# Attention, Fourier mixing and two channel mixers on one core: the softmax reciprocals go to the feature layout through TensorE, not through DRAM

## The chip, the cores and the metric

One core of a Trainium2 chip runs the whole kernel in one launch. The metric is device time in microseconds, median of three runs; less is better.

## What is computed

Three layers follow each other over 4 batches of 576 positions with 8 heads of 64 features (512 features in all). The change touches the end of the first one.

```python
scores = scale * np.matmul(q, k.transpose(0, 1, 3, 2)) + decay   # decay from the running sum of log f, causal
attn = np.exp(scores - np.max(scores, axis=-1, keepdims=True))
attn = attn / (np.sum(attn, axis=-1, keepdims=True) + 1e-09)
x = np.matmul(attn, v)                       # [B, H, S, D], then to [B, S, 512]
u = x + np.real(fft(fft(x, axis=1), axis=2))
x = u + np.maximum(layernorm(u) @ w_ch1, 0.0) @ w_ch2
theta = x @ w_theta                          # then the second mixer, cos, sin, token and channel weights
```

## The kernel before, in words

The kernel has three phases. Phase 1 is attention over 32 heads, in 16 pairs, with the Fourier layer of a batch woven in after its four pairs; phase 2 is the first channel mixer; phase 3 the second mixer. Only phase 1 is touched, and the profile shows attention from about 10 to 366 us.

For each head `score_units` works through five blocks of 128 queries (the last block is queries 448 to 575, of which the last 64 are new). TensorE makes scores in PSUM (L232, L233), VectorE masks them and takes the row minimum (L240), ScalarE exponentiates them into the tile `P` with the row sums as a by-product in `zs` (L245). After the second head of a pair VectorE adds the pieces of the sums and takes the reciprocals (L250 to L254), giving `rz`, with queries on partitions: `[128, 2 heads, 5 blocks]`. `turn_units` transposes the exponentials on TensorE (L275) and copies them out of PSUM with ScalarE (L279) or, for the first of four banks, VectorE (L281). `av_units` multiplies them with `v` in the PSUM tile `T` (L297), in which features of both heads lie on partitions and queries run along the row. So the scaling needs the reciprocals along the row, the same for 64 partitions at a time: the tile `R`, `[128, 576]`.

In the kernel before, `rz` gets there through DRAM. Four stores on SP's DMA queue (L257, L258) write one element at a time into `row`, two lines of 576 numbers; two loads (L485) read each line back with a broadcast to 64 partitions. They are issued at the start of the step that begins the product with `v`, two heads after the sums. `evac_pair` then multiplies `T` by `R` on VectorE into `X` (even pair, L313) or `Y` (odd pair, L319). For an odd pair three small copies on SP's queue move single rows of `Y` about (L322 to L329), GpSimd clears one row (L324), and GpSimd makes `E = X + Y` and `O = X - Y` (L332, L334), from which `fft_units` makes the Fourier layer.

SP's queue also carries, in the order of the program, the loads of heads (`raw`, L191, two buffers, 576 KB) and of `v` (L186). An instruction on that queue that waits holds those behind it. `prep_units` starts each head: ScalarE rounds `raw` to `hi` (L200), GpSimd takes the remainder (L201), and so on to L211, on VectorE.

A scheduler in the language orders the instructions of each engine, by emission and a priority: scores have 20 and the product with `v` 40 instructions of advance. The buffers that matter are `T` (one, of two PSUM banks), `R` (one), `X` (one), the slot `ol` (one, shared by `Y` and a tile of `fft_units`), and three PSUM banks of `bank_b`, which the transposes, the Fourier layer and the layer norm share. `phase1` advances the generators of transposes, product with `v` and scores in turn, about six rounds a head.

Of the kernel before, what the change touches and what calls it, by code (L numbers as in the profile page):

```python
# [8 lines left out]
F32 = mybir.dt.float32  # L9
# [4 lines left out]
ALU = mybir.AluOpType  # L14
# [3 lines left out]
B, H, S, D = 4, 8, 576, 64  # L18
NP = 4
# [36 lines left out]
class Net:  # L56
# [159 lines left out]
    def score_units(self, hd, g):  # L216
        nc = self.nc
        hi, kl, q2 = hd["hi"], hd["pair"]["kl"], self.q2[g]
        P = self.w3.tile([128, 1856], F32, tag="P", name="P", bufs=2)
        mn = self.w3.tile([128, 8], F32, tag="mn", name="mn", bufs=2)  # L220
        pr = hd["g"] // 2
        zs, rz = self.zs[pr % 2], self.rz[pr % 2]
        hd["P"] = P
        for i in (4, 3, 2, 1, 0):
            n0 = TOP[i]
            q = slice(n0, n0 + 128)
            ps = self.bank_a()
            pd = self.bank_a() if i == 4 else None
            parts = [(ps, 0, n0), (pd, n0, n0 + 128)] if i == 4 else [(ps, 0, n0 + 128)]
            with self.tc.high_priority(20):  # L230
                for t, a, b in parts:
                    nc.tensor.matmul(t[:, 0 : b - a], hi[:, 1, q], hi[:, 0, a:b], start=True, stop=False)  # L232
                    nc.tensor.matmul(t[:, 0 : b - a], q2[:, q], kl[:, g, a:b], start=False, stop=True)  # L233
                if i < 4:
                    dg, w, init = ps[:, 0 : n0 + 128], n0 + 128, 3.0e38
                else:
                    dg, w, init = pd[:, 0:128], 128, mn[:, 5:6]
                    nc.vector.tensor_reduce(init, ps[:, 0:n0], mybir.AxisListType.X, ALU.min)
                lowest = mn[:, i : i + 1]
                nc.vector.tensor_tensor_reduce(  # L240
                    out=dg, in0=dg, in1=self.mask[:, S - w : S], scale=1.0, scalar=init,
                    op0=ALU.add, op1=ALU.min, accum_out=lowest,
                )
                for k, (t, a, b) in enumerate(parts):
                    nc.scalar.activation(  # L245
                        P[:, POFF[i] + a : POFF[i] + b], t[:, 0 : b - a], AF.Exp, bias=lowest,
                        scale=-1.0, accum_out=zs[:, g, i + k : i + k + 1],
                    )
            if i == 0 and g:
                nc.vector.tensor_scalar(rz[:, :, 0:4], zs[:, :, 0:4], 1e-9, None, ALU.add)  # L250
                nc.vector.scalar_tensor_tensor(
                    rz[:, :, 4:5], zs[:, :, 4:5], 1e-9, zs[:, :, 5:6], ALU.add, ALU.add
                )
                nc.vector.reciprocal(rz[:, :, 0:5], rz[:, :, 0:5])  # L254
                row = self.fdram.tile([2, S], F32, tag="row", name="row", bufs=2)
                for k in range(2):
                    nc.sync.dma_start(row[k : k + 1, 0:512].rearrange("o (i p) -> p (o i)", p=128), rz[:, k, 0:4])  # L257
                    nc.sync.dma_start(row[k : k + 1, 512:S].rearrange("o p -> p o"), rz[64:128, k, 4:5])  # L258
                hd["pair"]["row"] = row
            yield  # L260

    def turn_units(self, hd):
# [18 lines left out]
                nc.vector.tensor_copy(dst, ps[:, 0:w])  # L281
            yield

    def av_units(self, hds, T, done):
        nc = self.nc
        v = hds[0]["pair"]["v"]
        place = {(j, a): PTOFF[bank] + off for bank, pieces in enumerate(TURNED) for j, a, b, off in pieces}
        yield
        for js in ((0, 1), (2, 3, 4)):
            with self.tc.high_priority(40):  # L290
                for j in js:
                    for lo_q, hi_q in ((0, 256), (256, 576)):
                        a = max(lo_q, 128 * j)
                        if a >= hi_q:
                            continue
                        for g, hd in enumerate(hds):
                            nc.tensor.matmul(  # L297
                                T[64 * g : 64 * g + 64, 256 + a : 256 + hi_q],
                                v[:, j, g, :],
                                hd["PT"][:, place[j, a] : place[j, a] + hi_q - a],  # L300
                                start=j == 0,
                                stop=j == 4 or (j == 1 and hi_q == 256),
                            )
            for _ in range(5 if js[0] == 0 else 1):
                yield
        done()

    def evac_pair(self, p, R, T):
        nc = self.nc
        k = p // 2  # L310
        if p % 2 == 0:
            self.X = self.c1.tile([128, S], F32, tag="X", name="X", bufs=1)
            nc.vector.tensor_tensor(self.X, T[:, 256:832], R, ALU.mult)  # L313
            if k == 0:
                self.EO = [self.c1.tile([128, 2, S], F32, tag=x, name=x, bufs=2) for x in ("E", "O")]
            return
        X, (E, O) = self.X, self.EO
        Y = self.c1.tile([128, S], F32, tag="ol", name="Y", bufs=1)
        nc.vector.tensor_tensor(Y, T[:, 256:832], R, ALU.mult)  # L319
        if k == 0:  # L320
            self.x384 = self.fdram.tile([1, S], F32, tag="x384", name="x384", bufs=2)
            nc.sync.dma_start(self.x384, Y[64:65])  # L322
            nc.sync.dma_start(Y[64:65], Y[0:1])
            nc.gpsimd.memset(Y[0:1], 0.0)  # L324
        else:
            self.x256 = self.c1.tile([1, S], F32, tag="x256", name="x256", bufs=1)
            nc.sync.dma_start(self.x256, Y[64:65])
            nc.sync.dma_start(Y[64:65], Y[0:1])
            nc.sync.dma_start(Y[0:1], self.x384)  # L329
        for _ in range(4):  # L330
            yield
        nc.gpsimd.tensor_tensor(E[:, k], X, Y, ALU.add)  # L332
        yield
        nc.gpsimd.tensor_tensor(O[:, k], X, Y, ALU.subtract)  # L334
        yield
# [104 lines left out]
    def phase1(self):  # L440
        pair, heads = self.p1_open()
        NH = B * H
        pairs, heads, raws = {0: pair}, dict(enumerate(heads)), {}
        fft = None
        self.tick = 0
        rows, norm, av = iter(()), iter(()), iter(())
# [19 lines left out]
        for n in range(-1, NH + 1):  # L466
# [13 lines left out]
            m, odd = divmod(n - 2, 2)  # L480
            if m >= 0 and not odd:
                T = self.bank_t()
                R = self.w3.tile([128, S], F32, tag="R", name="R", bufs=1)
                for k in range(2):
                    self.nc.sync.dma_start(R[64 * k : 64 * k + 64], pairs[m]["row"][k : k + 1].to_broadcast([64, S]))  # L485
                av = self.av_units([heads[2 * m], heads[2 * m + 1]], T, lambda m=m, T=T, R=R: done(m, T, R))
            t = self.turn_units(heads[n]) if 0 <= n < NH else iter(())
            if n == NH - 1:
                self.p1a.close()
# [692 lines left out]
```

## Time and profile before

| What | Value |
|---|---|
| Median of 3 runs | 1097.87 us (1094.99 to 1103.09) |
| Profiled execution, its time | 1099.61 us |
| Its span, first to last instruction | 1097.8 us |
| Mean granted TensorE clock | 0.937 |
| TensorE matmuls busy | 970.4 us (88%) |
| VectorE, ScalarE, GpSimd busy | 649.4, 450.8, 500.1 us |

The profile is one execution, taken apart by instruction. Times of rows are microseconds from the first instruction. A busy TensorE need not run at its full rate: the granted clock says how much of it the chip allowed, 1.00 or half of that at a time, and a mean between them says how the stretch was divided. Idle time of an engine is put down to what released it last. L numbers are lines of the kernel before.

### The profile page before, as it was taken

To read this page: it belongs to the slowest core of one execution; us is meant where nothing else is said; L and a number is where in the kernel's file an instruction comes from. 1 tells how busy PE (TensorE), PEld (TensorE's weight loads), DVE (VectorE), ACT (ScalarE), POOL (GpSimd) and SP (SyncE) were. 2 spreads that over 40 slices of the span, in tenths; PEclk is the share of its full clock that TensorE was granted. 3 is DMA by queue.
4 is the path that set the end of the run, shared out by engine and by line. 5 is a ranking of instruction groups with operands and counts; after the bars stand their busy time and mean duration, and the time that the engine had idled before them with its cause. 6 is when DMAs were issued, how large, how long until landed. Compare 5 with 4: busy or idle time off the path is not lost. (4 is left out here: it accounts for less than half of the span.)

```text
span 1097.8 us, 16258 instructions
## 1 busy us (share of the span) xinstructions
PE 970.4 (88%) x5880; PEld 874.3 (80%) x5880; DVE 649.4 (59%) x1429; ACT 450.8 (41%) x1128; POOL 500.1 (46%) x534
## 2 busy tenths in 40 slices
PE   4578898869879558999989999999999999999998
PEld 3355566546656347999989999999999999999998
DVE  7454765666756497875345533653467675665654
ACT  5355654554644443433123322422244453434431
POOL 5334523433535476664226541653266663635421
PEclk9878988979989777899999999999999999999999
DMA  4765444526343422100012123213342000000001
GB/s 148 121 119 89 112 63 93 98 69 79 71 74 46 88 77 69 48 1 5 35 40 100 53 86 108 77 54 126 116 143 66 1 1 23 22 23 23 12 33 44
DMA packets 46355, 72.85 MB, mean 66 GB/s; under 512 B 23502, under 2 KB 26958, under 8 KB 46276
## 3 DMA queue, kind: packets, MB, share of 16 engines
q1 hardware_dynamic: 42436, 67.32, 24.1%
q0 software_dynamic: 3120, 3.33, 2.3%
q10 hardware_dynamic: 720, 1.18, 0.3%
q8 instruction: 46, 0.75, 0.3%
q14 instruction: 33, 0.27, 0.1%
HBM read 62.64 MB, written 9.14 MB: 65 GB/s over the span
## 5 line engine op out<-in xcount | busy, mean ns | idle before, releaser
L740 PE MATMUL pa<-un,wf 128*128 128x384 f32 x1152 | 225.1, 343 | 24.2 <-POOL wf L568 12.5
L740 PEld LDWEIGHTS pa<-un,wf 128*128 128x128 f32 x1152 | 205.7, 192 | 27.6 <-POOL wf L568 13.6
L746 DVE SCALAR_TENSOR_TENSOR h<-pa,h 128x384 fp32r<-128x384 f32 x96 | 53.0, 555 | 166.7 <-ACT h L745 166.7
L754 PE MATMUL pb<-h,wf 128*128 128x384 f32 x660 | 138.2, 342 | 3.5 <-ACT h L745 3.1
L232 PE MATMUL pa<-hi 128*128 128x448 f32 (+2 forms) x192 | 77.6, 411 | 71.4 <-ACT P L245 58.0
L245 ACT ACTIVATE P<-pa,mn 128x512 f32<-128x512 f32 (+2 forms) x192 | 97.8, 517 | 89.4 <-DVE mn L240 65.8
L754 PEld LDWEIGHTS pb<-h,wf 128*128 128x128 f32 x660 | 118.7, 192 | 5.6 <-ACT h L745 3.8
L232 PEld LDWEIGHTS pa<-hi 128*128 128x128 f32 x192 | 41.8, 218 | 90.3 <-ACT P L245 56.1
L745 ACT ACTIVATE h<-pa 128x384 fp32r<-128x384 f32 x96 | 46.8, 489 | 154.6 <-PE pa L740 154.4
L754 PE MATMUL po<-h,wf 128*128 128x384 f32 x492 | 105.3, 343 | 2.5 <-DVE u L762 1.7
L961 PE MATMUL pb<-wtk,z 128*128 128x288 f32 x513 | 97.0, 294 | 0.0
L275 PE MATMUL pb<-ident,P 128*128 128x128 f32 x480 | 90.4, 307 | 6.4 <-DVE yl L392 6.0
L297 PE MATMUL pt<-PT,v 128*64 128x320 f32 (+4 forms) x448 | 94.5, 406 | 1.5 <-ACT PT L279 1.5
L951 POOL TENSOR_TENSOR z<-kra,z 128x256 fp32r<-128x256 f32 x72 | 53.9, 768 | 88.1 <-ACT z L950 88.1
L754 PEld LDWEIGHTS po<-h,wf 128*128 128x128 f32 x492 | 89.3, 193 | 4.0 <-ACT h L745 2.1
L565 POOL TENSOR_TENSOR a<-a,wf 128x512 f32<-128x512 f32 x32 | 42.2, 1321 | 106.7 <-DVE t L564 102.9
L275 PEld LDWEIGHTS pb<-ident,P 128*128 128x128 f32 x480 | 64.5, 156 | 28.8 <-issue 17.4
L240 DVE CUSTOM_DVE_ANT_0 pa<-pa,mask 128x512 f32<-128x512 f32 (+3 forms) x128 | 62.6, 504 | 36.6 <-PE pa L233 33.3
L961 PEld LDWEIGHTS pb<-wtk,z 128*128 128x128 f32 x513 | 79.2, 188 | 0.0
L961 PE MATMUL po<-wtk,z 128*128 128x288 f32 x351 | 75.1, 295 | 2.2 <-ACT z L950 1.6
L233 PE MATMUL pa<-kl,q 66*128 66x448 f32 (+2 forms) x192 | 68.8, 371 | 1.2 <-DVE kl L211 1.2
L201 POOL TENSOR_TENSOR hi<-raw,hi 64x576 fp32r<-64x576 f32 x31 | 45.4, 1466 | 45.1 <-ACT hi L200 40.5
(206 smaller groups left out, 1932.9 us busy)
## 6 DMA issues: line engine op xcount, KB each, us to landing
raw<-in_qk SPq DMA_DIRECT2D x31, 576.0 KB
raw<-in_wf SPq DMA_DIRECT2D x32, 512.0 KB
raw<-in_wtk SPq DMA_DIRECT2D x18, 288.0 KB
v<-in_vp SPq DMA_DIRECT2D x16, 320.0 KB
R<-row SPq DMA_DIRECT2D x32, 144.0 KB
out<-ob SPq DMA_DIRECT2D x12, 288.0 KB
dft<-in_dft POOLq DMA_DIRECT2D x8, 346.0 KB, 11.8
raw<-in_wth SPq DMA_DIRECT2D x4, 512.0 KB
```

What stands on the lines that cost most here:

```text
L232: nc.tensor.matmul(t[:, 0 : b - a], hi[:, 1, q], hi[:, 0, a:b], start=True, stop=False)
L233: nc.tensor.matmul(t[:, 0 : b - a], q2[:, q], kl[:, g, a:b], start=False, stop=True)
L240: nc.vector.tensor_tensor_reduce(out=dg, in0=dg, in1=self.mask[:, S - w : S], scale=1.0, scalar=init, op0=ALU.add, op1=ALU.min, accum_out= ...
L245: nc.scalar.activation(P[:, POFF[i] + a : POFF[i] + b], t[:, 0 : b - a], AF.Exp, bias=lowest, scale=-1.0, accum_out=zs[:, g, i + k : i + k ...
L275: nc.tensor.transpose(ps[:, o : o + 128], src, self.ident)
L297: nc.tensor.matmul(T[64 * g : 64 * g + 64, 256 + a : 256 + hi_q], v[:, j, g, :], hd["PT"][:, place[j, a] : place[j, a] + hi_q - a], start= ...
L740: nc.tensor.matmul(ps[:, 0:CH], t[:, l, 128 * d : 128 * d + 128], un[r][:, d], start=n == 0, stop=n == 11)
L745: nc.scalar.activation(h[:, 0], ps[:, 0:CH], AF.Relu)
L746: nc.vector.scalar_tensor_tensor(h[:, 1], ps[:, 0:CH], 0.0, f(h[:, 0]), ALU.max, ALU.subtract)
L754: nc.tensor.matmul(outs[d], t[:, l, 128 * d : 128 * d + 128], h[:, r], start=k % G == 0 and n == 0, stop=k % G == G - 1 and n == 2,)
L951: nc.gpsimd.tensor_tensor(z[:, 1], t, f(z[:, 0]), ALU.subtract)
L961: nc.tensor.matmul(acc[k][th], z[:, l, 128 * k : 128 * k + 128], self.wtk[kt][:, r, 288 * th : 288 * th + 288], start=first and i == 0 and ...
```

## The change

The stores, the tile `row` and the loads of `R` go. In `score_units`, after the reciprocals, GpSimd spreads `rz` into a new tile `wide`, `[128, 5 blocks, 128]`, in which each reciprocal of head 0 stands 64 times and each of head 1 64 times (one instruction, one buffer). In `av_units`, ahead of the second group of products with `v` of the pair, the new `spread` transposes the five blocks on TensorE, four of them into a bank of `bank_b` and the fifth into unused columns of `T`, and ScalarE copies them (512 columns and 64 columns) into `R`. `R` now stands in the slot of `X` or of `Y`, and the multiply of `evac_pair` writes over it.

```diff
--- before.py
+++ after.py
@@ -252,11 +252,12 @@
                     rz[:, :, 4:5], zs[:, :, 4:5], 1e-9, zs[:, :, 5:6], ALU.add, ALU.add
                 )
                 nc.vector.reciprocal(rz[:, :, 0:5], rz[:, :, 0:5])
-                row = self.fdram.tile([2, S], F32, tag="row", name="row", bufs=2)
-                for k in range(2):
-                    nc.sync.dma_start(row[k : k + 1, 0:512].rearrange("o (i p) -> p (o i)", p=128), rz[:, k, 0:4])
-                    nc.sync.dma_start(row[k : k + 1, 512:S].rearrange("o p -> p o"), rz[64:128, k, 4:5])
-                hd["pair"]["row"] = row
+                wide = self.w3.tile([128, 5, 128], F32, tag="wide", name="wide", bufs=1)
+                each = rz[:, :, 0:5].rearrange("p g i -> p i g").unsqueeze(3).to_broadcast([128, 5, 2, 64])
+                nc.gpsimd.tensor_scalar(
+                    wide.rearrange("p i (g c) -> p i g c", g=2), each, 1.0, 1.0, ALU.mult, ALU.mult
+                )
+                hd["pair"]["rz"] = wide
             yield
 
     def turn_units(self, hd):
@@ -281,12 +282,25 @@
                 nc.vector.tensor_copy(dst, ps[:, 0:w])
             yield
 
-    def av_units(self, hds, T, done):
+    def spread(self, p, T, wide):
+        nc = self.nc
+        R = self.c1.tile([128, S], F32, tag="ol" if p % 2 else "X", name="Y" if p % 2 else "X", bufs=1)
+        ps = self.bank_b()
+        for i in range(5):
+            to = T[:, 0:128] if i == 4 else ps[:, 128 * i : 128 * i + 128]
+            nc.tensor.transpose(to, wide[:, i], self.ident)
+        nc.scalar.copy(R[:, 0:512], ps)
+        nc.scalar.copy(R[:, 512:S], T[:, 64:128])
+        return R
+
+    def av_units(self, m, hds, T, wide, done):
         nc = self.nc
         v = hds[0]["pair"]["v"]
         place = {(j, a): PTOFF[bank] + off for bank, pieces in enumerate(TURNED) for j, a, b, off in pieces}
         yield
         for js in ((0, 1), (2, 3, 4)):
+            if js[0]:
+                R = self.spread(m % NP, T, wide)
             with self.tc.high_priority(40):
                 for j in js:
                     for lo_q, hi_q in ((0, 256), (256, 576)):
@@ -303,19 +317,19 @@
                             )
             for _ in range(5 if js[0] == 0 else 1):
                 yield
-        done()
+        done(m, T, R)
 
     def evac_pair(self, p, R, T):
         nc = self.nc
         k = p // 2
         if p % 2 == 0:
-            self.X = self.c1.tile([128, S], F32, tag="X", name="X", bufs=1)
-            nc.vector.tensor_tensor(self.X, T[:, 256:832], R, ALU.mult)
+            self.X = R
+            nc.vector.tensor_tensor(R, T[:, 256:832], R, ALU.mult)
             if k == 0:
                 self.EO = [self.c1.tile([128, 2, S], F32, tag=x, name=x, bufs=2) for x in ("E", "O")]
             return
         X, (E, O) = self.X, self.EO
-        Y = self.c1.tile([128, S], F32, tag="ol", name="Y", bufs=1)
+        Y = R
         nc.vector.tensor_tensor(Y, T[:, 256:832], R, ALU.mult)
         if k == 0:
             self.x384 = self.fdram.tile([1, S], F32, tag="x384", name="x384", bufs=2)
@@ -480,10 +494,7 @@
             m, odd = divmod(n - 2, 2)
             if m >= 0 and not odd:
                 T = self.bank_t()
-                R = self.w3.tile([128, S], F32, tag="R", name="R", bufs=1)
-                for k in range(2):
-                    self.nc.sync.dma_start(R[64 * k : 64 * k + 64], pairs[m]["row"][k : k + 1].to_broadcast([64, S]))
-                av = self.av_units([heads[2 * m], heads[2 * m + 1]], T, lambda m=m, T=T, R=R: done(m, T, R))
+                av = self.av_units(m, [heads[2 * m], heads[2 * m + 1]], T, pairs[m]["rz"], done)
             t = self.turn_units(heads[n]) if 0 <= n < NH else iter(())
             if n == NH - 1:
                 self.p1a.close()
```

## Rows read from the trace of the kernel before

**Rows 1.** the page: busy us (share of span) xinstructions by engine

```profile
PE 970.4 (88%) x5880; PEld 874.3 (80%) x5880; DVE 649.4 (59%) x1429; ACT 450.8 (41%) x1128; POOL 500.1 (46%) x534
```

**Rows 2.** windows: length, busy us of PE, PEld, DVE, ACT, POOL, granted clock

```profile
28.00:116.00 88.00, 63.10 (x334) 42.93 (x333) 43.10 (x127) 44.06 (x136) 33.48 (x35) 0.83 0.66 115
116.00:202.00 86.00, 75.14 (x415) 54.37 (x415) 52.87 (x143) 46.76 (x143) 34.75 (x39) 0.86 0.43 87
202.00:293.00 91.00, 72.48 (x417) 52.20 (x417) 56.08 (x145) 46.31 (x143) 33.40 (x37) 0.89 0.47 81
293.00:360.00 67.00, 56.95 (x321) 39.48 (x320) 42.34 (x115) 34.08 (x105) 29.99 (x34) 0.95 0.34 51
```

**Rows 3.** timeline of TensorE: start, us, instruction [idle before it <-releaser]

```profile
54.89 0.80 PE L232 MATMUL pa<-hi 128*128 128x512 f32 x1 [12.05 <-ACT P L245]
...
76.58 0.47 PE L232 MATMUL pa<-hi 128*128 128x128 f32 x1 [6.44 <-ACT P L245]
...
97.17 0.47 PE L232 MATMUL pa<-hi 128*128 128x128 f32 x1 [3.81 <-ACT P L245]
...
138.51 0.71 PE L232 MATMUL pa<-hi 128*128 128x448 f32 x1 [4.12 <-ACT P L245]
...
222.64 0.80 PE L232 MATMUL pa<-hi 128*128 128x512 f32 x1 [6.71 <-ACT P L245]
...
243.94 0.47 PE L275 MATMUL pb<-ident,P 128*128 128x128 f32 x1 [6.04 <-DVE yl L392]
...
276.51 0.44 PE L232 MATMUL pa<-hi 128*128 128x384 f32 x1 [3.21 <-ACT P L245]
...
312.90 0.47 PE L232 MATMUL pa<-hi 128*128 128x128 f32 x1 [6.18 <-ACT P L245]
```

**Rows 4.** timeline of VectorE, the multiply by R, same columns

```profile
53.32 0.76 DVE L313 TENSOR_TENSOR X<-pt,R 128x576 f32<-128x576 f32 x1 [12.18 <-DMA R<-row]
...
75.61 0.76 DVE L319 TENSOR_TENSOR Y<-pt,R 128x576 f32<-128x576 f32 x1 [8.02 <-DMA R<-row]
...
96.60 0.76 DVE L313 TENSOR_TENSOR X<-pt,R 128x576 f32<-128x576 f32 x1 [4.26 <-DMA R<-row]
```

**Rows 5.** timeline of ScalarE, the first rounding of a head

```profile
242.48 0.67 ACT L200 CAST hi<-raw 128x576 fp32r<-128x576 f32 x1 [6.70 <-DMA raw<-in_qk]
...
308.94 0.67 ACT L200 CAST hi<-raw 128x576 fp32r<-128x576 f32 x1 [5.62 <-DMA raw<-in_qk]
```

**Rows 6.** waits, 0 to 500 us: us in total, times, longest us

```profile
ACT hi L200 <- DMA raw<-in_qk: 35.0, 6, 8.4
...
POOL Y L324 <- DMA Y<-Y: 24.6, 3, 11.7
...
DVE X L313 <- POOL O L334: 8.0, 2, 6.6
```

**Rows 7.** waits of the SP queue, 0 to 500 us

```profile
SPq L485 <- DMA row<-rz: 98.3, 21, 9.2
```

**Rows 8.** timeline of the SP queue: last row store, next R loads

```profile
157.08 0.51 SPq L258 DMA_DIRECT2D row<-rz  x1
...
171.10 2.48 SPq L485 DMA_DIRECT2D R<-row  x2
```

**Rows 9.** the page: DMA packets by size

```profile
DMA packets 46355, 72.85 MB, mean 66 GB/s; under 512 B 23502, under 2 KB 26958, under 8 KB 46276
```

**Rows 10.** timeline of TensorE: runs of transposes, x is their number

```profile
68.63 1.09 PE L275 MATMUL pb<-ident,P 128*128 128x128 f32 x8
...
98.62 1.27 PE L275 MATMUL pb<-ident,P 128*128 128x128 f32 x5
```

**Rows 11.** window of the transposes alone: length, PE, PEld, clock, DMA

```profile
150.00:175.00 25.00, 5.13 (x32) 3.81 (x32) 1.00 0.52 48
```

**Rows 12.** lines by form, ScalarE, 28 to 375 us: count, busy, mean ns, idle

```profile
L279 ACT COPY PT<-pb 128x512 f32<-128x512 f32 x31 | 18.1, 584 | 10.9 <-PE pb L275 9.2 <-PE pa L233 1.5
```

**Rows 13.** lines by form, GpSimd, 28 to 375 us

```profile
L204 POOL TENSOR_SCALAR hi<-raw 128x576 fp32r<-128x576 f32 x7 | 4.7, 669 | 23.4 <-issue 14.6 <-PE pa L233 6.6 <-PE pa L232 2.2
```

## What was predicted

> **What bounds the kernel now.** I read the page first: TensorE is busy for 88% of the span and no other engine for more than 59% [rows 1]. That share is a mean over stages, so the next view is the windows over attention, the only stage that the change touches. From 28 to 360 us TensorE is busy for 63.10, 75.14, 72.48 and 56.95 us in windows of 88, 86, 91 and 67 us [rows 2], 267.7 of 332, so 64.3 us idle; its mean granted clock is 0.83 to 0.95, while no other engine reaches 64%. Attention is bound by TensorE with holes in it, and the question is who makes the holes.
>
> The timeline of TensorE has eight idle times of more than 3 us there [rows 3]. They sum to 12.05 + 6.44 + 3.81 + 4.12 + 6.71 + 6.04 + 3.21 + 6.18 = 48.6 us, three quarters of the 64.3. All are put down to ScalarE or VectorE, so the third step is to ask what those stood behind. Just before the first three VectorE stood for 12.18, 8.02 and 4.26 us in the multiply by R, until R had landed [rows 4]; masks and minima queue behind that multiply, the exponentials wait for the minima, and the scores for the PSUM banks. At the sixth and eighth hole ScalarE stood 6.70 and 5.62 us for the data of a head [rows 5]; six such waits sum to 35.0 us [rows 6]. The rest go back to E and O on GpSimd, which stood 24.6 us for the small copies of Y, and for which the X multiply stood 8.0 [rows 6].
>
> Heads and copies of Y share SP's queue with the stores and loads of the reciprocals. That queue stood 98.3 us in front of the R loads because the row stores had not landed, 9.2 us at the longest [rows 7]. One case: the last store is issued at 157.08 and the R loads only from 171.10 on [rows 8]. Head loads and copies behind them on the queue are issued later by as much. The row stores are also many: each pair writes 2 × (512 + 64) = 1152 single numbers, 16 pairs 18,432, which is most of the 23,502 packets under 512 B [rows 9].
>
> **What goes.** Six DMAs a pair, 96 in all, and the stand on SP's queue. I take the holes one kind at a time.
> - The first three, 22.3 us, end with R landing [rows 3, 4]. No DMA makes R afterwards: all of it goes.
> - The other five, 26.3 us, come from heads and copies of Y that are late [rows 3, 5, 6]. These DMAs remain, but no store of single numbers is in front of them. A head still waits for its buffer, and three copies of Y still follow one another, so not all goes. Bounds 0 and 26.3; I take 70%, 18 us.
> - The clock. Full and half speed are the two levels (2.4 and 1.2 GHz), so a mean c means a share 2(1 − c) at half: 29.9 + 24.1 + 20.0 + 6.7 = 80.7 us at half clock [rows 2]. If all 64.3 us of idle time lie in it, 16.4 us of work ran at half clock; if none, 80.7. Work at half clock costs half of its time, so 8 to 40 us are lost. Right after the third hole a run of transposes takes 0.25 us each, another run 0.14 [rows 10], so work behind a hole does run slowly. I put the loss near 18 us and give back two thirds with the holes: 12 us.
>
> Together −52 us.
>
> **What comes.**
> - TensorE: five transposes of 128x128 a pair, 80 in all. Eight in a run took 1.09 us, five took 1.27 us at the lower clock [rows 10]: 0.14 to 0.25 us each, 11 to 20 us. Between the holes TensorE is the bound, so it is paid in full; I take 14.
> - A rule speaks against this term. The Trainium skill (TensorE: Matmul & The Clock Gate, Part 4, PE-mode transpose) says that the full clock does not engage for transposes, which do not count as activity in the same way. The trace only half agrees: a window of 25 us with 32 transposes in it ran at a granted clock of 1.00 throughout [rows 11], with other matmuls between them. By the rule this term would be 20 us instead of 14.
> - ScalarE: copies of 512 and 64 columns from PSUM. The first takes 0.58 us [rows 12], the second between nothing and that: 0.58 to 1.17 us a pair, 9 to 19 in all, on an engine busy 44.06 of 88 us [rows 2]. If TensorE's remaining work covers it, it costs nothing; without cover all 19. Behind these copies stand exponentials, for which scores wait; I take 4.
> - GpSimd: one pass over 640 elements on 128 partitions. 576 elements took 0.67 us [rows 13], so 0.74 us, 12 in all; if the broadcast costs double, 24. GpSimd is busy 33.48 of 88 us [rows 2], so its idle time covers it: 0. Without that cover up to 24, since the remainder of the next head (L201) stands behind it. It also takes up a new wait, for the reciprocals and, with one buffer of wide, for the transposes of the pair before; the pair has two heads of time for it, so 0 again, within the same 24.
> - VectorE: the multiply now waits for two copies on ScalarE. They are emitted ahead of the last products with v, whose run covers them: 0. If the priority of the products puts the transposes behind them, that cover is gone and one copy chain a pair stays, 1.2 us × 16 = 19.
> - SP's queue is only relieved. It keeps heads, v and the copies of Y.
>
> Together +18 us. The sum is 1099.6 − 52 + 18 = 1065.6 us on the profiled execution, whose own time (1099.61) lies 1.7 us above the median of the runs (1097.87): 1064 us.
>
> **Rivals.**
> 1. *The holes go whole.* All eight holes and 30 us of the clock are won, the transposes run at the full clock and the copies are covered: −48.6 − 30 + 11 = −68, 1030 us. For it: SP's stand is 98.3 us, twice the holes [rows 7]. Against it: the buffers of raw and the chain of Y copies stay.
> 2. *Other waits fill the holes.* Only the three R holes go, with the price of their clock unrecovered because the chain scores, minimum, exponential refills the time: −22 + 18 = −4, 1094 us. For it: every hole is released by ScalarE or VectorE [rows 3], which the change does not speed up. Against it: those engines are busy for half to two thirds of the windows [rows 2] and were held by DMAs at the holes.
> 3. *Slower: the slot of R.* R now takes the slot of X or ol when the copy on ScalarE is written, not at the multiply. O of the pair before reads X and Y, so the copy can stand for it, on the engine of the exponentials. Before, VectorE stood at this place 8.0 us in two cases, 6.6 at the longest [rows 6]. If the 16 pairs stand 4.4 us each, that is 70 us: −52 + 18 + 70 = +36, 1134 us. It decides from 34 / 16 = 2.1 us a pair. Against it: O is late mostly through the copies of Y, 24.6 us of them [rows 6], and these come sooner.
> 4. *The clock does not come back.* The time won is filled with transposes and TensorE stays as long at the lower level: the transposes cost 20 us and the 12 us of clock are not won, −40 + 24 = −16, 1082 us. The window at 1.00 with 32 transposes in it speaks against it [rows 11]. The Trainium skill's rule on transposes (above) would give this case.
>
> **How the numbers follow.** Chances: forecast 0.52 (1045 to 1080), holes whole 0.15, other waits 0.13, no clock 0.10, slower 0.10. About 1% is what a measurement of this kernel can tell from no change. Faster by more, below 1086.9, are the forecast, the whole holes and the case without the clock: 0.77, and I leave 0.02 of that to the middle. Within 1%: other waits and that rest, 0.15. Slower: 0.10. The range leaves out the slow case and the upper part of the first rival: 1030 to 1096. It takes in the full 19 us of the copies or the 24 us of GpSimd on top of the sum (1083 or 1088). The likeliest case's own range is 1045 to 1080.
>
> **What would show it.** Right: no R loads in the waits, packets under 512 B near 23,502 − 18,432 = 5070, the wait of ScalarE for heads well under 35.0 us, GpSimd's wait for copies of Y under 10, the granted clock of the attention windows above 0.9, and the end of attention some 30 us earlier with the phases behind it unchanged in length. Wrong: new idle time on ScalarE before the copies into R released by O, or on GpSimd before wide released by the transposes; holes of TensorE of the old size with other releasers; a granted clock no higher although the holes are fewer.

## The result and the profile after

| | before | changed |
|---|---|---|
| median, same chip | 1100.11 us | 1014.61 us (1011.74 to 1016.53, 4 runs) |
| changed to before | | 0.9225, 95% interval 0.9180 to 0.9271 |
| the profiled execution, its span | 1099.61, 1097.8 us | 1011.74, 1010.0 us |

The kernel became 85.5 us faster; 34 were forecast (1064 against 1097.87), and 1014.61 lies below the range of 1030 to 1096. The direction is as predicted, and most of the gain lies in attention as predicted; the size is not.

The page of the changed kernel, engines and packets, beside [rows 1, 9] (PE is TensorE, PEld its loading of weights, DVE VectorE, ACT ScalarE, POOL GpSimd, SPq SP's queue):

```profile
PE 927.5 (92%) x5960; PEld 855.4 (85%) x5960; DVE 649.8 (64%) x1429; ACT 460.2 (46%) x1160; POOL 511.0 (51%) x550
...
DMA packets 24339, 68.06 MB, mean 67 GB/s; under 512 B 3534, under 2 KB 6990, under 8 KB 24260
```

TensorE's busy time fell by 42.9 us although it has 80 instructions more. Nothing that it did before was taken away, so its instructions became shorter or overlap more. The packets under 512 B fell by 19,968, more than the 18,432 numbers of the row stores; the other 1,536 are exactly 16 for each of the 96 DMAs that went. (Part 4 puts 64 of these DMAs back, and 19,456 packets under 512 B with them: the 18,432 numbers and again 16 for each DMA.)

Two windows of the changed kernel, from 28 us to the last product with v and from there to the end (columns: length; busy us of PE, PEld, DVE, ACT, POOL, each with its count; granted clock, DMA share, GB/s):

```profile
28.00:294.50 266.50, 238.83 (x1621) 180.18 (x1620) 199.68 (x540) 189.03 (x575) 146.41 (x164) 0.99 0.32 97
294.50:1010.00 715.50, 676.47 (x4295) 664.91 (x4294) 429.64 (x846) 254.57 (x545) 350.61 (x354) 0.97 0.16 53
```

The same two of the kernel before, whose last product with v ends at 370.8 us, somewhat later than the end of attention named ahead of the prediction:

```profile
28.00:370.80 342.80, 277.28 (x1536) 196.30 (x1535) 197.91 (x534) 176.84 (x538) 135.64 (x148) 0.87 0.48 85
370.80:1097.80 727.00, 681.36 (x4299) 668.28 (x4299) 431.40 (x850) 257.15 (x550) 350.41 (x354) 0.97 0.17 55
```

Attention went from 342.8 to 266.5 us, 76.3 of the 87.8 us by which the span is shorter. There TensorE's idle time went from 65.5 to 27.7 us, its busy time from 277.28 to 238.83 us with 85 instructions more (the 80 transposes; a few records are missing from a trace), and its granted clock from 0.87 to 0.99. The stages behind are 11.5 us shorter. (The changed kernel was profiled a second time, with every engine's instructions in the same order: attention was 267.0 us and the stages behind 718.5, so a difference of 3 us between two profiles means nothing.)

The waits of the changed kernel, 0 to 420 us (us in total, times, longest us):

```profile
ACT P L245 <- DVE mn L240: 59.5, 43, 7.6
...
POOL Y L338 <- DMA Y<-Y: 3.5, 2, 2.4
...
ACT X L292 <- POOL O L348: 3.5, 3, 1.8
POOL wide L257 <- PE pb L291: 3.4, 3, 2.6
```

ScalarE's wait for a head's data, 35.0 us before [rows 6], is no longer among them: what ScalarE waits for most is the minima of VectorE, 59.5 us, that is the computation itself. All that is left of a wait for a head is 0.4 us on GpSimd, once. GpSimd's wait for the copies of Y fell from 24.6 to 3.5 us. Two waits are new: the copy into R for O of the pair before (3.5 us; the second copy, L293, adds 1.1) and wide for the transposes of the pair before (3.4). SP's queue of the changed kernel, same stretch and columns:

```profile
SPq L191 <- DVE kl L211: 117.7, 27, 10.1
...
SPq L343 <- DMA Y<-Y: 8.0, 3, 2.9
```

SP stands 117.7 us, longer than the 98.3 of [rows 7], but for buffers that are still in use: it is ahead of its work now.

### The profile page after: what moved, and what is told of

Same layout as the page of the kernel before. It is cut to its first block, busy times and chain, and to the rows that moved or that the text cites. A ratio compares the mean times of both kernels' runs of the same rounds, so it can differ in the third digit from the quotient of the medians.

```text
span 1010.0 us, 16314 instructions
## 1 busy us (share of the span) xinstructions
PE 927.5 (92%) x5960; PEld 855.4 (85%) x5960; DVE 649.8 (64%) x1429; ACT 460.2 (46%) x1160; POOL 511.0 (51%) x550
## 2 busy tenths in 40 slices
DMA packets 24339, 68.06 MB, mean 67 GB/s; under 512 B 3534, under 2 KB 6990, under 8 KB 24260
## 5 line engine op out<-in xcount | busy, mean ns | idle before, releaser
L765 PE MATMUL pb<-h,wf 128*128 128x384 f32 x660 | 135.5, 338 | 2.6 <-ACT h L756 2.3
L245 ACT ACTIVATE P<-pa,mn 128x512 f32<-128x512 f32 (+3 forms) x192 | 98.7, 520 | 62.3 <-DVE mn L240 59.5
L232 PE MATMUL pa<-hi 128*128 128x448 f32 (+2 forms) x192 | 72.4, 387 | 29.1 <-ACT P L245 17.4
L972 PE MATMUL pb<-wtk,z 128*128 128x288 f32 x513 | 98.3, 297 | 0.0
L576 POOL TENSOR_TENSOR a<-a,wf 128x512 f32<-128x512 f32 x32 | 42.9, 1343 | 96.2 <-DVE t L575 96.2
L276 PE MATMUL pb<-ident,P 128*128 128x128 f32 x480 | 84.3, 284 | 4.9 <-ACT X L292 1.9
L240 DVE CUSTOM_DVE_ANT_0 pa<-pa,mask 128x256 f32<-128x256 f32 (+3 forms) x128 | 61.6, 502 | 23.8 <-PE pa L233 21.1
L232 PEld LDWEIGHTS pa<-hi 128*128 128x128 f32 x192 | 38.1, 200 | 44.6 <-ACT P L245 19.8
L276 PEld LDWEIGHTS pb<-ident,P 128*128 128x128 f32 x480 | 58.7, 144 | 15.3 <-issue 4.3
L311 PE MATMUL pt<-PT,v 128*64 128x320 f32 (+4 forms) x448 | 64.6, 369 | 6.2 <-ACT X L293 3.8
L233 PE MATMUL pa<-kl,q 66*128 66x448 f32 (+2 forms) x192 | 64.5, 354 | 1.5 <-DVE kl L211 1.5
L936 PE MATMUL pa<-wf,xs 128*128 128x256 f32 x456 | 63.9, 289 | 0.0
```

What stands on the lines that cost most here:

```text
L240: nc.vector.tensor_tensor_reduce(out=dg, in0=dg, in1=self.mask[:, S - w : S], scale=1.0, scalar=init, op0=ALU.add, op1=ALU.min, accum_out= ...
L245: nc.scalar.activation(P[:, POFF[i] + a : POFF[i] + b], t[:, 0 : b - a], AF.Exp, bias=lowest, scale=-1.0, accum_out=zs[:, g, i + k : i + k ...
L276: nc.tensor.transpose(ps[:, o : o + 128], src, self.ident)
L311: nc.tensor.matmul(T[64 * g : 64 * g + 64, 256 + a : 256 + hi_q], v[:, j, g, :], hd["PT"][:, place[j, a] : place[j, a] + hi_q - a], start= ...
L765: nc.tensor.matmul(outs[d], t[:, l, 128 * d : 128 * d + 128], h[:, r], start=k % G == 0 and n == 0, stop=k % G == G - 1 and n == 2,)
L936: nc.tensor.matmul(th, xs[:, l, d], self.wth[d][:, r, 256 * hf : 256 * hf + 256], start=n == 0, stop=n == 11)
```

## The experiments

The question was why more than twice as much came back. Theories: the transport's stores cost more than the stand that I counted; the clock gives back more; the new code makes TensorE's own work shorter. Ratios are to runs of the kernel before on the same chip, taken beside each kernel. The changed kernel was also run again, unedited, beside later ones:

> The changed kernel as it is, beside the other two on the same chip: 1010 to 1018 us.

Measured: 1016.36 us, 0.9269 (0.9245 to 0.9292); the mean of the changed kernel's two ratios is 0.9247. Below, differences of ratios are turned into us at 1098 us.

### 1. The transport alone, and what takes its place

> The kernel before without any transport: no row stores, no loads of R, and the multiply uses a constant tile in place of the reciprocals, so the scaling of attention is left out. The products stand apart, as before. Theory 1: as fast as the changed kernel or faster by what its transposes and copies cost, 995 to 1015 us. Theory 2: slower than the changed kernel although it does less, 1020 to 1040 us.

```diff
-                for k in range(2):
-                    nc.sync.dma_start(row[...], rz[:, k, 0:4])
-                    nc.sync.dma_start(row[...], rz[64:128, k, 4:5])
...
-                    self.nc.sync.dma_start(R[64 * k : 64 * k + 64], pairs[m]["row"]...)
+                R = self.fixed
```

Here R is a constant of 1/256 and nothing of the reciprocals is carried or spread. Measured: 1020.37 us, 0.9268 (0.9230 to 0.9305), at the lower edge of the second theory. The same two windows of this kernel:

```profile
28.00:297.40 269.40, 251.49 (x1534) 177.91 (x1534) 194.61 (x534) 175.68 (x539) 134.92 (x146) 0.99 0.31 92
297.40:1017.30 719.90, 679.82 (x4299) 667.12 (x4299) 431.70 (x851) 257.07 (x551) 354.24 (x356) 0.97 0.16 54
```

Against the kernel before, idle time in attention fell by 47.6 us (65.5 to 17.9) and busy time by 25.8 us (277.28 to 251.49), with 1534 instructions for 1536. The clock went from 0.87 to 0.99, so the same work runs faster. That this is the clock shows on the transposes of the exponentials, which no edit touches (before, then constant R; count, busy us, mean ns of one):

```profile
L275 PE MATMUL pb<-ident,P 128*128 128x128 f32 x461 | 86.4, 305 | 6.4 <-DVE yl L392 6.0 <-ACT PT L279 0.2 <-DVE PT L281 0.2
```

```profile
L272 PE MATMUL pb<-ident,P 128*128 128x128 f32 x460 | 81.1, 281 | 1.0 <-DVE PT L278 0.8
```

The shortest (270 ns) and the median (273 ns) are the same in both kernels; only the longest go, 476 against 330 ns. By the clock records of the trace of before, its 83 transposes at half clock took a median of 421 ns, the 377 at the full clock 273. So the 25.8 us are the clock term, all but what the other order of instructions adds or takes. Behind attention 7.1 us went. Removing the transport thus gives 80.5 us of span. Yet the changed kernel, which pays for 80 transposes and 32 copies more, isn't slower than this one (0.9247 against 0.9268). Something in it gives about as much back as these cost.

### 2. Products that gather

TensorE's lines in attention, the products with v and the new transposes (count, busy us, mean ns of one, idle before and its releasers); the changed kernel, then the kernel before, then the one with the constant R:

```profile
L311 PE MATMUL pt<-PT,v 128*64 128x320 f32 (+4 forms) x448 | 64.6, 369 | 6.2 <-ACT X L293 3.8 <-DVE X L327 0.9 <-ACT PT L280 0.7
...
L291 PE MATMUL pb<-ident,wide 128*128 128x128 f32 x64 | 10.9, 274 | 0.0
```

```profile
L297 PE MATMUL pt<-PT,v 128*64 128x320 f32 (+4 forms) x448 | 94.5, 406 | 1.5 <-ACT PT L279 1.5
```

```profile
L294 PE MATMUL pt<-PT,v 128*64 128x320 f32 (+4 forms) x448 | 86.6, 373 | 1.5 <-ACT PT L276 1.5
```

The same 448 products took 94.5, 86.6 and 64.6 us. From constant R to changed kernel that is −22.0 us at one clock (0.99), more than the transposes cost: 14.3 us for all 80, the 16 into T included, which have a row of their own. (Rows of lines that stand among one another overlap in time, so these figures don't add up to TensorE's busy time. Counted without overlap, each matmul from its own start to the start of the next, the products went from 78.7 to 60.7 us and the transposes took 9.9.) TensorE's timeline of the kernel before (start, us, instruction, number in a run) shows the second group of a pair's products, five of six pieces:

```profile
87.81 0.75 PE L297 MATMUL pt<-PT,v 128*64 128x320 f32 x2
...
88.94 0.54 PE L297 MATMUL pt<-PT,v 128*64 128x192 f32 x2
...
89.67 0.54 PE L297 MATMUL pt<-PT,v 128*64 128x192 f32 x2
...
90.56 0.33 PE L297 MATMUL pt<-PT,v 128*64 128x64 f32 x2
...
91.25 0.33 PE L297 MATMUL pt<-PT,v 128*64 128x64 f32 x2
```

And of the changed kernel:

```profile
75.80 1.20 PE L311 MATMUL pt<-PT,v 128*64 128x320 f32 x12
...
107.30 1.48 PE L311 MATMUL pt<-PT,v 128*64 128x320 f32 x12 [2.40 <-ACT X L293]
```

Before, pieces came one by one between other matmuls: 2.49 us for ten instructions. In the changed kernel all twelve stand in one run of 1.20 us. The releaser in the second row tells why: the copy of T[:, 64:128] on ScalarE (L293) holds the second group until it is done, and then all its pieces are ready. That an uninterrupted run is cheaper agrees with the Trainium skill (TensorEngine Tiling (Array Packing), Tiling Modes, Key Properties): a switch of the tiling mode drains TensorE, and the products here (128x64) stand between matmuls of 128x128. No run here shows the drain itself, nor whether the halves of a run overlap.

Four kernels give the second group that wait or take it away. First the changed kernel with the fifth block in a bank of its own, so that nothing holds the products:

> The changed kernel with the fifth block of reciprocals transposed into a PSUM bank of its own, so that the products with v wait for no copy of T and stand apart in TensorE's order, as in the kernel before. Theory 1: no change, 1012 to 1020 us. Theory 2: 26 us slower than the changed kernel, 1036 to 1046 us.

```diff
+        pf = self.bank_b()
...
-            to = T[:, 0:128] if i == 4 else ps[:, 128 * i : 128 * i + 128]
+            to = pf[:, 0:128] if i == 4 else ps[:, 128 * i : 128 * i + 128]
```

Measured: 1039.13 us, 0.9439 (0.9402 to 0.9477), 21 us slower than the changed kernel, near the second theory. Its products, its window of attention and the waits of the turning transposes (those of the exponentials):

```profile
L312 PE MATMUL pt<-PT,v 128*64 128x320 f32 (+4 forms) x448 | 86.3, 388 | 2.8 <-DVE X L328 1.5 <-ACT PT L280 0.7 <-DVE Y L334 0.5
```

```profile
28.00:321.00 293.00, 268.93 (x1613) 190.40 (x1611) 200.29 (x539) 188.57 (x574) 146.60 (x164) 0.95 0.29 88
```

```profile
PE pb L276 <- ACT X L293: 4.3, 3, 2.3
PE pb L276 <- DVE PT L282: 3.8, 6, 1.5
```

Products are back at 86.3 us. But the extra bank also costs: TensorE's transposes wait for banks (4.3 and 3.8 us), and the clock is 0.95. So the 21 us can have two parts, and the next kernels add the gathering alone, by one useless transpose into T and a small copy out of it ahead of the second group: to that kernel, to the one with the constant R, and to the kernel before.

```diff
+            if js[0]:
+                junk = self.w3.tile([128, 64], F32, ...)
+                nc.tensor.transpose(T[:, 0:128], self.ident, self.ident)
+                nc.scalar.copy(junk, T[:, 64:128])
```

> The kernel with the fifth block in a PSUM bank of its own, and the products gathered again by one more transpose and one more small copy (not used). If the 24 us that the bank of its own cost came from products standing apart: back to 1014 to 1022 us. If they came from the shortage of PSUM banks (two of three held at once): it stays at 1036 to 1044 us.

> The same without transport (the scaling of attention is left out), and the products gathered by one transpose and one small copy. Theory 1: the time of the kernel without transport and with products apart, or 1 to 3 us more. Theory 2: 26 us less than that kernel, 990 to 1010 us. Against the changed kernel both theories read from it what the transposes, the copies and the pass on GpSimd cost: 5 to 20 us.

> The kernel before, its way through DRAM kept, with one thing of the changed kernel added: ahead of the second group of products with v one transpose into the unused columns of T and one small copy of T on ScalarE, so that the six products of the group become ready at once and stand together in TensorE's order. The copied numbers are not used. Theory 1 (all of the gain comes from the DMAs): no gain, 1098 to 1106 us. Theory 2 (neighbouring products of two heads run together: 1.20 us for a group of the changed kernel, 2.8 us for the six pieces of before): 16 x 1.6 = 26 us faster, 1070 to 1082 us, less where a hole swallows it.

| gathering added to | us | ratio | interval | difference | products |
|---|---|---|---|---|---|
| own bank | 1027.56 | 0.9363 | 0.9339 to 0.9386 | −8 us | 86.3 to 71.5 us |
| constant R | 1012.78 | 0.9197 | 0.9155 to 0.9239 | −8 us | 86.6 to 72.3 us |
| kernel before | 1102.66 | 1.0019 | 0.9988 to 1.0050 | +2 us, within the noise | 94.5 to 70.2 us |

The first lies between its two expectations, back to the changed kernel or no gain, and the second between its two, no gain or 26 us; the third is as the first theory has it. The row and window of the constant R with gathering, and those of the kernel before with it:

```profile
L298 PE MATMUL pt<-PT,v 128*64 128x320 f32 (+4 forms) x448 | 72.3, 391 | 6.9 <-issue 3.7 <-ACT PT L276 1.6 <-ACT junk L290 1.3
```

```profile
28.00:295.50 267.50, 241.85 (x1563) 178.14 (x1561) 194.98 (x540) 179.91 (x559) 137.18 (x148) 0.96 0.32 95
```

```profile
L301 PE MATMUL pt<-PT,v 128*64 128x320 f32 (+4 forms) x448 | 70.2, 391 | 14.7 <-ACT junk L293 10.1 <-DVE X L317 2.7 <-ACT PT L279 1.5
```

```profile
28.00:378.60 350.60, 254.32 (x1564) 191.43 (x1562) 194.36 (x542) 182.06 (x562) 136.97 (x149) 0.87 0.61 86
```

Each time the products become 14 to 24 us shorter, and 8 us of it reaches the end where the transport is gone (clear of noise with the own bank; with the constant R the two intervals just touch). The rest goes into waiting: with the constant R idle time in attention rises by 7.7 us (17.9 to 25.6), 5.4 of it before the products themselves (1.5 to 6.9). In the kernel before none of it reaches the end: busy time falls from 277.28 to 254.32 us, but idle time rises from 65.5 to 96.3. Some of that is the new copy, for which the products stand 10.1 us, and ScalarE's wait for heads grows from 35.0 to 44.0 us (0 to 500 us); where the rest comes from isn't shown. So in this kernel gathering gained something only once the transport was gone. The 13 us between the own bank with gathering and the changed kernel remain for the bank and the extra transposes and copies, not split further.

The constant R with gathering also gives the price of what the change adds besides: the changed kernel (0.9247) is 5 to 6 us slower than it (0.9197), at the low end of the 5 to 20 us expected for the other transposes, the wide copies and the pass on GpSimd.

Then the spread's bank taken from the banks of the scores instead of those of the turning transposes:

> The changed kernel with the four transposed blocks in a PSUM bank of the scores (bank_a) in place of one of the transposes (bank_b). If the three banks of bank_b are still what is short in the changed kernel: 3 to 8 us faster, 1006 to 1011 us. If scores run short instead: 3 to 10 us slower.

```diff
-        ps = self.bank_b()
+        ps = self.bank_a()
```

Measured: 1020.72 us, 0.9322 (0.9297 to 0.9347), about 6 us slower than the changed kernel beside it (1016.36 us). The bank of the turning transposes is the better place, by little.

### 3. The price of the transposes

> The changed kernel with every one of the five transposes of the reciprocals done twice, into the same place (80 more transposes in all). If a transpose is paid in full on TensorE, as I took it: 80 x 0.11 to 0.17 = 9 to 14 us more, 1024 to 1029 us. If idle time of TensorE covers it: 1014 to 1018 us.

```diff
-        for i in range(5):
+        for i in (0, 1, 2, 3, 0, 1, 2, 3, 4, 4):
```

Measured: 1021.43 us, 0.9317 (0.9300 to 0.9333), 5 to 10 us more than the changed kernel by its two ratios, between the two expectations. 80 more transposes cost 0.07 to 0.13 us each; TensorE is busy with them for 12.2 us more (14.3 to 26.5), so most of that is paid, but not shown to be paid in full. (The 274 ns in the line above are the duration of one, and those of a run overlap.)

### 4. What the stores cost when nobody waits for them

> The changed kernel with the row stores of before put back, which nobody waits for and nobody reads (4 stores of single numbers a pair on SP's queue, no loads of R). Theory 1a (the cost of the way through DRAM is SP's queue standing until the rows have landed, and VectorE standing for R): nearly the changed kernel, 1014 to 1024 us. Theory 1b (the single numbers themselves hold up the loads of heads and the copies of Y on the DMA engines): 1035 to 1060 us.

```diff
+                row = self.fdram.tile([2, S], F32, tag="row", name="row", bufs=2)
+                for k in range(2):
+                    nc.sync.dma_start(row[k : k + 1, 0:512].rearrange("o (i p) -> p (o i)", p=128), rz[:, k, 0:4])
+                    nc.sync.dma_start(row[k : k + 1, 512:S].rearrange("o p -> p o"), rz[64:128, k, 4:5])
```

This is the changed kernel with the four row stores of before put back; no load follows, nothing is done with them. Measured: 1068.98 us, 0.9754 (0.9730 to 0.9778): 56 us slower than the changed kernel, two thirds of the whole gain, without a wait for the row stores on any computing engine (SP's queue stands 7.4 us for them, in three cases), and above the 1035 to 1060 us of the second theory.

Its DMA issues (KB each, median us from issue to landing) and its waits, 28 to 300 and 0 to 370 us:

```profile
raw<-in_qk SPq DMA_DIRECT2D x27, 576.0 KB, 8.7
...
row<-rz SPq DMA_DIRECT2D x28, 2.0 KB, 10.4
...
x<-Y SPq DMA_DIRECT2D x6, 2.2 KB, 9.5
```

```profile
ACT hi L200 <- DMA raw<-in_qk: 31.7, 7, 7.2
...
POOL xx L372 <- DMA x<-Y: 25.5, 3, 8.8
```

A row store of 2.0 KB takes 10.4 us to land, and others land late beside it: a head (576 KB) after 8.7 us and x, one of the copies of rows of Y, after 9.5. The changed kernel's own two rows:

```profile
raw<-in_qk SPq DMA_DIRECT2D x27, 576.0 KB, 3.9
...
x<-Y SPq DMA_DIRECT2D x8, 2.2 KB, 2.3
```

The waits of [rows 6] for heads are back, 31.7 us. Now the stand of SP for the row stores, added to this kernel by read-backs of half a row whose data isn't used:

> The changed kernel with the row stores and with two loads a pair that read half of each row back into a tile nobody reads, at the place in the program where R was loaded. So SP's queue stands until the rows have landed, as before, but no engine waits for R. Theory 1a: heads and copies of Y are issued late, 1040 to 1065 us. Theory 1b: within 8 us of the run with the stores alone. What remains up to the kernel before is VectorE's wait for R, with the clock behind it, and the order of the products.

```diff
+                back = self.w3.tile([128, 288], F32, ...)
+                for k in range(2):
+                    self.nc.sync.dma_start(back[64 * k : 64 * k + 64], pairs[m]["row"][k : k + 1, 0:288]...)
```

Measured: 1082.63 us, 0.9875 (0.9843 to 0.9908): 13 us more, which neither expectation gave. SP's waits of this kernel:

```profile
SPq L504 <- DMA row<-rz: 115.2, 25, 9.0
```

The stand is somewhat longer than before, 115.2 us for the 98.3 of [rows 7], and costs 13 us on top of the stores, the traffic of the read-backs (72 KB each) included. What is left to the kernel before, 14 us, holds the wait of the multiply for R, the products apart and the work in the other order, less what the change adds on TensorE, ScalarE and GpSimd; no run splits it.

### 5. What makes the stores dear

Is it their number, or where the numbers lie? All four kernels of this part are the one with the stores, with another layout in DRAM. First the stores as runs of 16 B (four numbers of a partition together, at a pitch of 40 B), which also makes fewer packets:

> The changed kernel with four stores of the reciprocals a pair that nobody waits for and nobody reads, on SP's queue like the stores of single numbers, of the same bytes, but with four numbers of a partition in one run of 16 bytes: 384 runs a pair in place of 1152. If the price of the stores (58 us with single numbers) goes by the number of runs: a third of it, some 20 us, 1028 to 1038 us. If it goes by the four DMAs and their time on SP's queue: 1060 to 1072 us.

```diff
-                row = self.fdram.tile([2, S], F32, ...)
+                row = self.fdram.tile([128, 2, 5], F32, ...)
...
+                    nc.sync.dma_start(row[:, k, 0:4], rz[:, k, 0:4])
+                    nc.sync.dma_start(row[64:128, k, 4:5], rz[64:128, k, 4:5])
```

Then the same single numbers, as many packets, but each 512, 64 or 16 B from the next:

> The changed kernel with the stores of single numbers that nobody waits for (1152 numbers a pair, as in the run that cost 56 us), but each number 512 bytes from the next in DRAM in place of beside it; the order of the instructions is the same on every engine. If the price goes by the number of single-number writes: again 1060 to 1075 us, stores landing after 10 us. If it comes from neighbouring numbers falling into the same piece of DRAM: 1015 to 1035 us, stores landing after 2 to 4 us.

> The same stores of 1152 single numbers a pair that nobody waits for, each number 64 bytes from the next in DRAM (512 bytes cost 4 us, side by side cost 56 us; runs of 16 bytes at a distance of 40 bytes cost 3 us). If writes hold one another up within pieces of 512 bytes: 8 numbers share one in place of 128, so most of the price is back, 1030 to 1070 us. If the piece is 64 bytes or less: 1015 to 1022 us, stores landing after 2 to 3 us.

> The same with 16 bytes from one number to the next. With a piece of 64 bytes 4 numbers share one in place of 16: something between, 1020 to 1045 us. With a piece of 32 bytes, 2 share one: 1015 to 1030 us. If only numbers side by side count: 1015 to 1020 us.

```diff
-                row = self.fdram.tile([2, S], F32, ...)
+                row = self.fdram.tile([2, S, 128], F32, ...)
...
-    row[k : k + 1, 0:512]
+    row[k : k + 1, 0:512, 0]
```

| numbers in DRAM | us | ratio | interval | row store lands after |
|---|---|---|---|---|
| side by side (part 4) | 1068.98 | 0.9754 | 0.9730 to 0.9778 | 10.4 us |
| 16 B apart | 1021.75 | 0.9318 | 0.9272 to 0.9364 | 3.8 us |
| 64 B apart | 1017.69 | 0.9295 | 0.9241 to 0.9349 | 2.3 us |
| 512 B apart | 1017.75 | 0.9290 | 0.9274 to 0.9305 | 2.3 us |
| runs of 16 B | 1019.17 | 0.9295 | 0.9264 to 0.9326 | 2.1 us |
| no stores (changed, again) | 1016.36 | 0.9269 | 0.9245 to 0.9292 | |

The packets on the page, side by side and 512 B apart:

```profile
DMA packets 43796, 68.15 MB, mean 64 GB/s; under 512 B 22990, under 2 KB 26446, under 8 KB 43716
```

```profile
DMA packets 43796, 68.15 MB, mean 67 GB/s; under 512 B 22990, under 2 KB 26446, under 8 KB 43716
```

The counts of packets are the same, and every engine has the same instructions in the same order in both kernels; only addresses in DRAM differ. Yet 51 us lie between them. The runs of 16 B lie below both of their expectations, and the numbers 16 B apart just above the one for which only numbers side by side count. The DMA rows 512 B apart, and then 16 B apart (28 to 300 us):

```profile
raw<-in_qk SPq DMA_DIRECT2D x27, 576.0 KB, 3.9
...
row<-rz SPq DMA_DIRECT2D x31, 2.0 KB, 2.3
```

```profile
raw<-in_qk SPq DMA_DIRECT2D x27, 576.0 KB, 4.4
...
row<-rz SPq DMA_DIRECT2D x32, 2.0 KB, 3.8
```

With 512 B the head lands after 3.9 us, as in the changed kernel. By the packet records of the traces the numbers themselves pass as quickly side by side as 512 B apart, a median of 9 and 8 ns a packet; what takes longer beside them are the packets of the heads (4,608 B), a mean of 388 against 231 ns. So neither the number of packets nor their size is dear, but numbers written side by side into DRAM, and most of that is gone at 16 B. The Trainium skill (DMA: Bandwidth & Descriptors, Specifications) has transfers under 512 B done as read-modify-write. This agrees in part at most: every packet of a row store here is under 512 B, and only the close ones are dear. Why close ones are, no run shows.

## Why the prediction was wrong

It is clearest on the spans of the profiled executions: before to constant R is what goes, constant R to changed kernel what comes.

| | forecast | measured |
|---|---|---|
| idle time that goes | −40 (22.3 + 18) | −47.6 |
| clock | −12 | −25.8 |
| behind attention | 0 | −7.1 |
| what comes, in all | +18 | −7.3 |
| of it TensorE | +14 | −12.7: transposes +14.3, products −22.0, the rest, with the overlap of these rows, −5.0 |
| of it idle time in attention | +4 | +9.8 |
| of it behind attention | 0 | −4.4 |
| sum | −34 | −87.8 |

These are single executions, and that of the changed kernel was its fastest. By the ratios of all runs what goes is 80 us (0.9268) in place of 52, and what comes is −2 us (0.9247 against 0.9268, within the noise) in place of +18.

**The holes: right.** I took the first three whole and 70% of the other five. In the changed kernel next to nothing waits for a head's data (0.4 us), and the idle time that went, 47.6 us, is nearly that of all eight holes, 48.6. Leaving 30% of the five to heads that still wait for buffers was too cautious by 7.6 us.

**Its reason: only half right.** I laid the late heads on SP's stand [rows 7], and gave the "many" stores a row [rows 9] but no price. The stores alone cost 56 us and bring 31.7 of the 35.0 us of late heads back, without the stand; the stand on top of them costs 13. So heads were late above all because the stores were in flight beside them. It didn't change the forecast for holes much, since both go together here; it would have for a change that removes only the stand.

**The clock: the first step that failed, and the term mis-sized most in what goes, 12 us for 25.8.** The bounds of 8 to 40 us held; inside them I took 18 and two thirds of it. The same instructions without holes took 25.8 us less, and the clock is 0.99 rather than 0.87. From 0.87, 2 × 0.13 × 342.8 = 89 us were at half clock; by the trace 65 us of them were work, where 18 us lost would have meant 36. That work at half clock costs half of its time is itself too much: a transpose took 421 ns there for 273 (part 1), a good third. I judged by a single run of slow transposes behind a hole [rows 10] and then took a further third off without a row for it.

**The transposes: right in busy time, 14.3 us for 14, but not paid in full.** 80 more cost 5 to 10 us, and all that the change adds besides the gathering 5 to 6 (part 2) where I had 18. The rule of the Trainium skill quoted in the prediction isn't borne out here: attention, now with the 80 transposes in it, ran at 0.99.

**The second step that failed: "what comes" is nothing, or a small gain, in place of +18 us.** I listed only costs, because the change only adds work to TensorE, ScalarE and GpSimd. I saw that the transpose into T stands ahead of the second group of products and that the multiply must wait for copies. But I didn't ask what the second group does when it is held: its pieces become ready together. The products with v, which no edit touches, lost 22.0 us by their own row, and the runs with the gathering alone are 8 us faster. I had put this at nothing. The trace of before had the sign of it: their row at 94.5 us for 448, in pieces of 0.33 to 0.75 us [the rows of experiment 2]. I hadn't read that row at all, since the diff doesn't touch L297's work.

**ScalarE, GpSimd, VectorE: nearly free, as taken.** GpSimd's pass takes 727 ns, 740 forecast; the copies some 583 and 226 ns. Idle time of TensorE rose by 9.8 us against the constant R, 3.8 of it before the products that wait for L293. The gathering alone raised it by 7.7 (part 2), so most of it is the price of gathering.

**Rivals.** The first (all holes, 30 us of clock, 1030 us) has the right mechanisms and nearly the right sizes, −47.6 and −25.8 for −48.6 and −30; what it lacks is the gathering and the 11.5 us behind attention. *Other waits fill the holes* falls: the longest idle time of TensorE in attention, from 28 us on, is now the 2.40 us shown above, before L311. *The slot of R* exists, but as 4.6 us over all pairs (3.5 + 1.1), far under the 34 from which it decides. *The clock does not come back* falls with 0.99.

**The signs.** The waits for heads and for copies of Y and the clock came as named. But 3,534 packets under 512 B are left, not 5070, for the 16 that go with each DMA; attention ends 76 us earlier, not 30; and the phases behind it are not unchanged. Of the signs of being wrong the two new waits came, at 4.6 and 3.4 us.

**Left open.** The stages behind attention became 7.1 us shorter with the constant R and 11.5 us with the change. Their code is the same, but the scheduler puts instructions in another order when anything changes, and no experiment holds that order fixed except those of part 5; two profiles of the changed kernel differ by 3 us there. All other differences of a few us carry this doubt.

## What to carry to other kernels

Numbers scattered singly into DRAM side by side are dear even when nobody waits for them, since the large loads beside them land late; if such a trip must stay, try the numbers 16 to 64 B apart. A hole of TensorE is to be priced twice, for itself and for the clock behind it: here 47.6 us of idle time less brought 25.8 us more. When a new wait is put ahead of a group of small matmuls, ask also whether it makes them run together, and read the row of that group's time even if the diff doesn't touch it.

## What was not expected of the hardware

- Single numbers of 4 B stored side by side land after 10.4 us, 16 B apart after 3.8, 64 or 512 B apart after 2.3, with the same packets; a head's load of 576 KB beside them lands after 8.7 us or 3.9. For this kernel that is 51 us.
- 448 products with 64-column halves take 94.5, 86.6 or 64.6 us, by how they stand among 128-column matmuls and by the clock (0.87, 0.99, 0.99). The gathering itself is worth 8 us at the end, and nothing while the transport is there.
- Beside the numbers of the row stores, 1,536 more small packets went with the 96 DMAs, 16 for each; 64 DMAs put back brought 1,024.
